# Outer products of a linear attention on half of the matmul array, and a new order of matmuls in a feed-forward block

## The chip, the cores and the metric

One NeuronCore of a Trainium2 chip runs the whole program. Its engines work through their own instruction queues side by side: PE (TensorE, the matmul array; PEld are its weight loads), ACT (ScalarE), DVE (VectorE), POOL (GpSimd) and SP, which here only issues DMAs. The metric is the time of one execution on the device in microseconds; before the change the median of three runs is 203.42 us (203.08 to 203.95).

## What is computed

A recurrent attention with decay feeds a two-layer network with a Mish activation.

```python
# q, k, v: (4, 8, 768, 64) fp32 (batch, heads, tokens, head size)
gamma = 1.0 - 2.0 ** (-5.0 - np.arange(H))
for t in range(S):
    state = gamma * state + outer(k[:, :, t], v[:, :, t])      # 64 x 64 per batch and head
    y[:, :, t] = scale * q[:, :, t] @ state
x = y.transpose(0, 2, 1, 3).reshape(3072, 512)
h = x @ w_in                                                    # (512, 2048)
out = (h * np.tanh(softplus(h))) @ w_out                        # (2048, 512), fp32 result
```

## The kernel before

The 3072 tokens are cut into 24 chunks of 128 (six to a batch). Two chunks make a block; the first block has four, so there are eleven blocks, 0 to 10. Of a chunk the attention is computed in a closed form, with the powers of the decay folded into q and v when they are cast to 16 bits:

- *scores* (`scores`, line 393): k times q within the chunk, per head, 16 matmuls for two chunks; `mask` (line 399) multiplies them by a triangle on DVE and gives `am`.
- *present* (line 443): v times `am`, the part of the output that comes from the chunk's own tokens. Each matmul has 64 weight columns, so that two heads lie in the two halves of the array.
- *outer* (line 407): k times v, summed over the chunk's tokens. Two heads lie side by side in one 128x128 product, of which only the two 64x64 squares on the diagonal are wanted; four matmuls a chunk.
- *state*: `state_sum` (line 419) adds the state of the chunk before on DVE, `state_decay` (line 424) multiplies by `gcm`, which holds the decay on the diagonal squares and zero elsewhere. The state is thus a 128x512 tile per chunk with zeros off the diagonal, and goes into
- *past* (line 433) as 128x128 weights: the part of the output that comes from earlier chunks, four matmuls a chunk.

`y_two` runs past and then present for the two chunks of a block into one PSUM tile `y_ps`, and ACT casts the result to `xt` (line 489), the input of the network.

Block 0 and the second product of block 1 are computed plainly, matmul by matmul, with the attention of the next block put between by a dictionary of steps (`plan` in `first_block`, `plan_of`). From there on both matrix products of a block go by a scheme of seven products in place of eight on quarters of the matrices: `g1_seven` (first product, with Mish; half of its units are seven-product quarters, line 639, half are `plain` units, line 663) and `seven` (second product, line 734). Both keep partial sums in three PSUM tiles `pb`, `px`, `pe`; `snap` copies one out on ACT (lines 646, 740), `plus` and `done` add on DVE (lines 656, 748). `x_sums`, `sums_a`, `sums_b` and `sums_c` form the sums of inputs on DVE that the scheme wants. A plain unit computes two columns of 128 and its Mish follows it at once.

The order of all instructions is the order in which the program is written; every engine takes its own in that order. The attention of the next block (nb) is put between by named steps: `steps_of(blk)` gives for each name the work that is issued there. In `g1_seven` the steps are p2, u2, p6, p7, p4, h2 and end, in `seven` m1, m2, m7 and m3. Before the change, p2 holds the next block's outer products (`outer_next`), the first sum and, on POOL, its decay; p7 the second sum; m2 the second decay; h2 the scores; m7 `y_two`. The casts of q and v on POOL, the loads of k by POOL's DMA queue (`bring_k`) and the transposing loads by SP (`turn_by_dma`) run two blocks ahead. `gate` is a small copy on POOL that makes the work behind it wait for sums on DVE.

PSUM is split into two pools: `mm` has four tiles for the network, `at` two for scores, outer products and `y_ps`.

Of the kernel before, what the change touches and what calls it, by code (L numbers as in the profile page):

```python
# [16 lines left out]
def kernel(  # L17
# [64 lines left out]
    tri = cpool.tile([P, C], FP32, name="tri")  # L82
    gcm = cpool.tile([P, HP, P], FP32, name="gcm")
    warm = cpool.tile([P, 1], FP32, name="warm")
    gate_t = cpool.tile([P, 1], FP16, name="gate")
# [19 lines left out]
    for h in range(H):  # L105
        o = 64 * (h % 2)
        nc.vector.memset(gcm[o:o + 64, h // 2, o:o + 64], float(gamma[h] ** C))

    win_ap = moe_w_in.rearrange("(bp p) f -> p bp f", p=P)
# [3 lines left out]
    raw, k16s, v16s, t16s, kts, amf = {}, {}, {}, {}, {}, {}  # L113
    loaded, cast, qkts, ats, ams, states, us, ys, sus = {}, {}, {}, {}, {}, {}, {}, {}, {}
    xts, gts, wins, wouts, wtmps = {}, {}, {}, {}, {}
# [10 lines left out]
    def room(g):  # L126
        loaded[g] = [
            lpool.tile([P, H, D], FP32, name=nm + "f", tag=nm + "f", bufs=4 if nm == "q" else 6)
            if g < BRING or nm != "k" else None for nm in "qkv"]
# [93 lines left out]
    def load_two(nm, s, half):  # L223
        t = lpool.tile([P, HP, R, D], FP32, name=nm + "f", tag=nm + "f", bufs=6)
# [179 lines left out]
    def outer(g, u_ps):  # L404
        _, k16, v16, _ = cast[g]
        for i in range(HP):
            nc.tensor.matmul(  # L407
                u_ps[:, i], k16[:, 2 * i:2 * i + 2], v16[:, 2 * i:2 * i + 2],
                start=True, stop=True)
        us[g] = u_ps  # L410

    def state_sum(g):
        u_ps = us.pop(g)
        if g % NCH == 0:
            states[g] = stp.tile([P, HP, P], FP16, name="st")
            nc.vector.tensor_tensor(states[g], u_ps, gcm, op=ALU.mult)
        else:
            sus[g] = stp.tile([P, HP, P], FP32, name="su")
            nc.vector.tensor_tensor(sus[g], u_ps, states[g - 1], op=ALU.add)  # L419

    def state_decay(g, by):
        if g in sus:
            states[g] = stp.tile([P, HP, P], FP16, name="st")
            by.tensor_tensor(states[g], sus.pop(g), gcm, op=ALU.mult)  # L424

    def state(g):
        state_sum(g)
        state_decay(g, nc.vector)

    def past(g, y, fresh, pairs=range(HP)):  # L430
        st, qt = states[g - 1], qkts[g][0]
        for i in pairs:
            nc.tensor.matmul(  # L433
                y(i), st[:, i], qt[:, i], start=fresh(i), stop=False,
                skip_group_check=True)

    def present(g, y, fresh, pairs=range(HP)):
        am = ams[g]
        v16 = cast[g][2]
        for i in pairs:  # L440
            for hh in range(2):
                o = 64 * hh
                nc.tensor.matmul(  # L443
                    y(i)[o:o + 64], v16[:, 2 * i + hh], am[:, hh, i],
                    start=fresh(i), stop=True, skip_group_check=True)

# [5 lines left out]
    def scores_one(g):  # L452
        scores(g)
        mask(g)

    def outer_state(g):
        outer(g, atps.tile([P, 2, HP, P], FP32, name="u_ps", tag="at")[:, 0])
        state(g)

# [9 lines left out]
    def outer_two(blk):  # L469
        a = first[blk]  # L470
        u_ps = atps.tile([P, 2, HP, P], FP32, name="u_ps", tag="at")
        for j in range(2):
            if not last_of_batch(a + j):
                outer(a + j, u_ps[:, j])
        for j in range(2):
            if not last_of_batch(a + j):
                state(a + j)

    def y_two(blk):
        a = first[blk]  # L480
        y_ps = atps.tile([P, HP, 2, C], FP32, name="y_ps", tag="at")
        inter = a % NCH > 0
        if inter:
            past(a, lambda i: y_ps[:, i, 0], lambda i: i % 2 == 0)
        past(a + 1, lambda i: y_ps[:, i, 1], lambda i: not inter and i % 2 == 0)
        for j in range(2):
            present(a + j, lambda i: y_ps[:, i, j], lambda i: False)
        xts[blk] = xtp.tile([P, HP, TB], FP16, name="xt")
        nc.scalar.copy(  # L489
            xts[blk][:, :, :2 * C], y_ps.rearrange("p i j c -> p i (j c)"))  # L490
# [125 lines left out]

    def g1_seven(blk, steps, sum_first=False):
        n = NBP // 2
# [40 lines left out]
        def plain(s, half):  # L659
            h_ps = mmps.tile([P, 2, 2 * P], FP32, name="h_ps", tag="mm")  # L660
            for j in range(2):
                for bp in range(NBP):
                    nc.tensor.matmul(  # L663
                        h_ps[:, j], win(s, 2 * half + j, bp), xt(blk, bp),
                        start=bp == 0, stop=bp == NBP - 1)
            fb = s * FPS + 2 * half
            nc.scalar.activation(gt[:, fb:fb + 2], h_ps, AF.Mish, scale=inv_boost3)  # L667
# [33 lines left out]
        plain(1, 1)  # L701
        step("h2")
        plain(3, 1)
        step("end")
# [9 lines left out]
    def seven(blk, steps, last):  # L714
# [51 lines left out]
        sums_c(blk)  # L766
        mm(pe, s(1), t(1), True)
        m5 = snap(pe)
        mm(px, s(3), t(3))
# [41 lines left out]
    def first_block():  # L811
# [72 lines left out]
        for s in range(1, NSL):  # L884
# [47 lines left out]

    def outer_next(blk):
        a = first[blk]
        u_ps = atps.tile([P, 2, HP, P], FP32, name="u_ps", tag="at")
        for j in range(2):
            if not last_of_batch(a + j):
                outer(a + j, u_ps[:, j])

    def sum_next(blk, j):  # L940
        if not last_of_batch(first[blk] + j):
            state_sum(first[blk] + j)

    def decay_next(blk, j):
        state_decay(first[blk] + j, nc.gpsimd)

# [49 lines left out]
    for blk in range(1, len(BLOCKS)):  # L996
        if blk >= SEVEN:
            steps = steps_of(blk)
            g1_seven(blk, steps, blk + 1 < len(BLOCKS) and not last_of_batch(first[blk + 1] + 1))
            seven(blk, steps, blk + 1 == len(BLOCKS))  # L1000
            continue
# [47 lines left out]
```

## Time and profile before

| what | us |
|---|---|
| median of three runs | 203.42 |
| the profiled execution's own time | 204.0 |
| its span, from the first to the last instruction | 202.2 |
| PE busy in it | 193.7 |
| DVE busy | 143.9 |
| ACT busy | 102.6 |
| POOL busy | 82.4 |
| outer products, line 407, 64 matmuls, busy | 5.2 |
| present, line 443, 160 matmuls, busy | 6.4 |
| sums of states on DVE, line 419, 13 | 8.9 |
| decays on POOL, line 424, 11 | 13.9 |

The profile is one execution. A busy time is the union of an engine's instructions; a matmul is shown with its full length, though the next one starts before it ends, so the spacing of starts says what a matmul costs. In the view of the chain, each piece is named by the engine and the line that the end of the program was waiting for at that time. In the timeline, a row gives the start of a merged piece, its length, the engine, the line and the operation, what is written and read, and how many instructions lie in it; square brackets name idle time ahead of it and what ended it.

### The profile page before, as it was taken

How to read it: one execution, taken by the hardware profiler on the slowest of the kernel's cores; microseconds unless marked ns; L12 is line 12 of the kernel's file. 1: busy time of each engine (PE TensorE's matmuls, PEld its weight loads, DVE VectorE, ACT ScalarE, POOL GpSimd, SP SyncE). 2: the span in 40 equal slices, each digit the busy share in tenths (PEclk: the TensorE clock that was granted, in tenths of full speed). 3: DMA queues.
4: the chain of work that ended last, by engine and by line, in shares of the span. 5: the costliest groups of instructions: out<-in, count | busy, mean ns of one | idle time of the engine just before them, and what ended most of it. 6: DMA issues, size and time to landing. Idle time of an engine off the chain costs nothing.

```text
span 202.2 us, 5401 instructions
## 1 busy us (share of the span) xinstructions
PE 193.7 (96%) x2239; PEld 153.0 (76%) x2239; DVE 143.9 (71%) x271; ACT 102.6 (51%) x183; POOL 82.4 (41%) x99
## 2 busy tenths in 40 slices
PE   6897999989999999999999999999999999999993
PEld 2455544445865888988988988988988988989982
DVE  2777693969848687588696696787696696596552
ACT  2363664151960572673573573563663753753840
POOL 4072000617645347646608629626609716200000
PEclk9999999999999999999999999999999999999999
DMA  5999999999899999999991998999992992200202
GB/s 163 303 312 357 386 386 305 270 255 194 150 116 273 253 201 202 144 176 211 188 183 49 151 165 174 167 172 156 209 200 62 186 136 56 105 3 28 80 26 78
DMA packets 95896, 36.55 MB, mean 181 GB/s; under 512 B 82304, under 2 KB 89984, under 8 KB 95872
## 3 DMA queue, kind: packets, MB, share of 16 engines
q1 hardware_dynamic: 75968, 33.30, 73.1%
q0 software_dynamic: 16640, 2.10, 16.4%
q10 hardware_dynamic: 3264, 0.82, 2.3%
q8 instruction: 17, 0.28, 0.6%
q14 instruction: 7, 0.06, 0.1%
HBM read 27.30 MB, written 6.29 MB: 166 GB/s over the span
## 4 chain that ended last, share of the span: by engine, by line
PE 80%; DMA 8%; DVE 6%; ACT 2%; issue 1%; SPq 0%; DVEq 0%
PE o_ps L734 28%; PE h_ps L663 18%; PE h_ps L639 16%; DMA wt<-in_moe_w_out_dram 6%; PE o_ps L526 6%; PE y_ps L443 3%; PE at L393 3%; DMA qfirst<-in_q_dram 2%; PE y_ps L433 2%; PE u_ps L407 2%; DVE tmat L558 1%; PE h_ps L807 1%; ACT xt L489 1%; DVE tmat L560 1%; DVE tmat L559 1%
## 5 line engine op out<-in xcount | busy, mean ns | idle before, releaser
L663 PE MATMUL h_ps<-xt,win 128*128 128x256 f16 x320 | 41.2, 273 | 0.0
L330 POOL TENSOR_TENSOR qk<-qf,qvs 128x512 f16<-128x512 f32 x20 | 24.0, 1199 | 25.5 <-DMA qf<-in_q_dram 25.3
L663 PEld LDWEIGHTS <-win 128*128 128x128 f16 x320 | 29.4, 98 | 3.6
L734 PEld LDWEIGHTS <-gsum 128*128 128x128 f16 x288 | 27.5, 98 | 3.8
L656 DVE TENSOR_TENSOR hsum<-h_ps,hsnap 128x512 f32<-128x512 f32 x30 | 19.8, 688 | 13.7 <-PE h_ps L639 11.4
L399 DVE TENSOR_TENSOR am<-at,tri 128x1024 f16<-128x1024 f32 x20 | 24.2, 1217 | 3.6 <-PE at L393 3.6
L667 ACT ACTIVATE g<-h_ps 128x512 f16<-128x512 f32 x40 | 23.8, 594 | 5.6 <-PE h_ps L663 5.5
L646 ACT COPY hsnap<-h_ps 128x512 f32<-128x512 f32 x30 | 16.6, 588 | 17.6 <-PE h_ps L639 17.6
L734 PE MATMUL o_ps<-tmat,gsum 128*128 128x256 f16 x216 | 25.1, 273 | 0.0
L345 POOL TENSOR_TENSOR v<-vf,qvs 128x512 f16<-128x512 f32 x20 | 21.3, 1063 | 5.2 <-DMA vf<-in_v_dram 5.2
L734 PEld LDWEIGHTS <-g 128*128 128x128 f16 x216 | 21.1, 98 | 2.4
L748 DVE TENSOR_TENSOR osb<-o_ps,snap 128x256 f32<-128x256 f32 x27 | 11.4, 424 | 16.0 <-PE o_ps L734 11.3
L526 PE MATMUL o_ps<-wout,g 128*128 128x512 f16 x96 | 22.7, 379 | 0.0
L489 ACT CAST xt<-y_ps 128x1024 f16<-128x1024 f32 x10 | 10.1, 1012 | 21.9 <-PE y_ps L443 21.9
L650 ACT ACTIVATE g<-hsum 128x512 f16<-128x512 f32 x30 | 18.7, 634 | 4.0 <-DVE hsum L656 4.0
L740 ACT COPY snap<-o_ps 128x256 f32<-128x256 f32 x27 | 10.1, 373 | 19.4 <-PE o_ps L734 19.4
L639 PEld LDWEIGHTS <-wsum 128*128 128x128 f16 x320 | 19.1, 98 | 0.5
L734 PE MATMUL o_ps<-wout,g 128*128 128x256 f16 x144 | 17.2, 273 | 0.0
L354 POOL COPY gate<-gsum 128x1 f16<-128x1 f16 x8 | 1.5, 183 | 37.9 <-DVE gsum L708 37.9
L639 PE MATMUL h_ps<-xsum,wsum 128*128 128x128 f16 x240 | 16.6, 219 | 0.0
L424 POOL TENSOR_TENSOR st<-su,gcm 128x512 f16<-128x512 f32 x11 | 13.9, 1267 | 6.1 <-DVE su L419 6.1
L639 PEld LDWEIGHTS <-win 128*128 128x128 f16 x240 | 15.1, 98 | 1.5 <-issue 0.8
(97 smaller groups left out, 294.0 us busy)
## 6 DMA issues: line engine op xcount, KB each, us to landing
vf<-in_v_dram SPq DMA_DIRECT2D x23, 256.0 KB, 5.7
out_dram<-osb SPq DMA_DIRECT2D x22, 256.0 KB, 4.9
qf<-in_q_dram SPq DMA_DIRECT2D x19, 256.0 KB, 5.5
wt<-in_moe_w_out_dram SPq DMA_DIRECT2D x3, 1024.0 KB, 9.2
wi<-in_moe_w_in_dram SPq DMA_DIRECT2D x4, 512.0 KB, 7.4
wi<-in_moe_w_in_dram SPq DMA_DIRECT2D x2, 1024.0 KB, 11.7
qk<-in_k_dram POOLq DMA_DIRECT2D x16, 128.0 KB, 5.4
kf<-in_k_dram SPq DMA_DIRECT2D x7, 256.0 KB, 6.0
```

What stands on the lines that cost most here:

```text
L330: nc.gpsimd.tensor_tensor(room16(g)[0], loaded[g][0], qs.unsqueeze(2).broadcast_to((P, H, D)), op=ALU.mult)
L345: nc.gpsimd.tensor_tensor(room16(g)[2], loaded[g][2], vs.unsqueeze(2).broadcast_to((P, H, D)), op=ALU.mult)
L399: nc.vector.tensor_tensor(am, ats.pop(g), tri.unsqueeze(1).unsqueeze(1).broadcast_to((P, 2, HP, C)), op=ALU.mult)
L424: by.tensor_tensor(states[g], sus.pop(g), gcm, op=ALU.mult)
L526: nc.tensor.matmul(o_ps, gts[blk, fb][:, t * P:(t + 1) * P], wouts[s][:, f, cols], start=(fb == 0), stop=(fb == NFB - 1))
L639: nc.tensor.matmul(h_ps[:, f], w(f, d), x(d), start=first and f == 0 and d == 0, stop=d == n - 1, skip_group_check=True)
L646: nc.scalar.copy(x, h_ps)
L650: nc.scalar.activation(gt[:, 2 * i * FPS:(2 * i + 1) * FPS, j * P:(j + 1) * P], h, AF.Mish, scale=inv_boost3)
L656: nc.vector.tensor_tensor(h, h_ps, x, op=ALU.add)
L663: nc.tensor.matmul(h_ps[:, j], win(s, 2 * half + j, bp), xt(blk, bp), start=bp == 0, stop=bp == NBP - 1)
L667: nc.scalar.activation(gt[:, fb:fb + 2], h_ps, AF.Mish, scale=inv_boost3)
L734: nc.tensor.matmul(o_ps, x(f), w(f), start=first and f == 0, stop=f == n - 1, skip_group_check=True)
```

## The change

Three things change together.

*Outer products and states.* `outer` computes each head alone: eight matmuls a chunk with 64 weight columns and 64 moving columns, the two heads of a pair in the two halves of the array. The result is compact, 128x256 with no zeros. `state_sum` and `state_decay` work on this compact form; `gcv` holds the decay as one column per pair of heads. `spread_state` then has ACT copy the two halves of partitions into a 128x512 tile (`stx`, three of them, whose zeros off the diagonal are set once at the start). One chunk, the fifth, keeps the wide form (`outer_wide`).

*Where they stand.* `y_two` now runs present first, then the outer products of the block's second chunk and of the next block's first (`outer_two`, `handed_on`; the last chunk of a batch has none), then past. The sums and decays follow in the steps of the next block's `g1_seven` and `seven`: sum and decay of one chunk at p2 with its spread at p7, sum of the other at p7, decay at m2 and spread at a new step m5. In block 0's plan `y_two` and in block 1's plan `outer_state` both compute the outer product of the seventh chunk.

*The first product.* `g1_seven` now issues a plain unit behind each pair of seven-product quarters; the Mish of a plain unit is issued later than its matmuls. The load buffers of k go from six to four.

```diff
     def outer(g, u_ps):
         _, k16, v16, _ = cast[g]
         for i in range(HP):
+            for hh in range(2):
+                nc.tensor.matmul(
+                    u_ps[64 * hh:64 * hh + 64, i], k16[:, 2 * i + hh], v16[:, 2 * i + hh],
+                    start=i == 0, stop=True, skip_group_check=True)
+        us[g] = u_ps
+
+    def state_sum(g):
+        u_ps = us.pop(g)
+        if g % NCH == 0:
+            stcs[g] = stp.tile([P, HP, D], FP16, name="stc", tag="stc")
+            nc.vector.tensor_tensor(stcs[g], u_ps, decay, op=ALU.mult)
+        else:
+            sus[g] = stp.tile([P, HP, D], FP32, name="suc", tag="suc")
+            nc.vector.tensor_tensor(sus[g], u_ps, stcs[g - 1], op=ALU.add)
+
+    def state_decay(g, by):
+        if g in sus:
+            stcs[g] = stp.tile([P, HP, D], FP16, name="stc", tag="stc")
+            by.tensor_tensor(stcs[g], sus.pop(g), decay, op=ALU.mult)
+
+    def spread_state(g):
+        states[g] = stx[g % 3]
+        for hh in range(2):
+            o = slice(64 * hh, 64 * hh + 64)
+            nc.scalar.copy(states[g][o, :, o], stcs[g][o])
...
     def y_two(blk):
         a = first[blk]
         y_ps = atps.tile([P, HP, 2, C], FP32, name="y_ps", tag="at")
-        inter = a % NCH > 0
-        if inter:
-            past(a, lambda i: y_ps[:, i, 0], lambda i: i % 2 == 0)
-        past(a + 1, lambda i: y_ps[:, i, 1], lambda i: not inter and i % 2 == 0)
         for j in range(2):
-            present(a + j, lambda i: y_ps[:, i, j], lambda i: False)
+            present(a + j, lambda i: y_ps[:, i, j], j == 0)
+        outer_two(blk)
+        for j in range(2):
+            if (a + j) % NCH > 0:
+                past(a + j, lambda i: y_ps[:, i, j])
...
         step("p2")
-        if sum_first:
-            mm(px, s(2), t(2))
-            u2 = snap(px)
+        h0 = plain(1, 0)
+        mm(px, s(2), t(2))
+        mish_of(0, 0, c11)
+        u2 = snap(px)
         mm(pe, s(1), t(1), True)
         m5 = snap(pe)
-        if not sum_first:
-            mm(px, s(2), t(2))
-            u2 = snap(px)
+        mish_plain(1, 0, h0)
         step("u2")
-        mish_of(0, 0, c11)
         step("p6")
-        plain(1, 0)
+        h1 = plain(3, 0)
         mm(px, s(3), t(3))
         c22 = plus(px, m5)
         mm(pe, s(4), b(1, 1))
         c12 = plus(pe, u2)
+        mish_plain(3, 0, h1)
         mish_of(1, 1, c22)
         mish_of(0, 1, c12)
         step("p7")
-        plain(3, 0)
+        h2 = plain(1, 1)
+        mish_plain(1, 1, h2)
         mm(px, a(1, 1), t(4))
         mish_of(1, 0, px)
         step("p4")
-        plain(1, 1)
         step("h2")
-        plain(3, 1)
+        h3 = plain(3, 1)
+        mish_plain(3, 1, h3)
         step("end")
...
-            28: [(outer_state, CPB), (casts, CPB + 2), (turn_and_load, CPB + 2), (cast_q, CPB + 3)],
+            28: [(outer_wide, CPB), (casts, CPB + 2), (turn_and_load, CPB + 2), (cast_q, CPB + 3)],
...
-            "p2": [*then((gate_x, blk), (cast_q, a)), *only((outer_next, nb), (sum_next, nb, 0),
-                   (decay_next, nb, 0)), (cast_v, a), (bring_k, a + 1)],
+            "p2": [*then((gate_x, blk), (cast_q, a)), (sum_next, a - 3), (decay_next, a - 3),
+                   (cast_v, a), (bring_k, a + 1)],
...
-            "p7": [(store_due, 2), *only((sum_next, nb, 1)), (sums_a, blk, slice(0, FPS))],
+            "p7": [(store_due, 2), (sum_next, a - 2), (spread_next, a - 3), (sums_a, blk, slice(0, FPS))],
...
-            "m2": [*only((gate_g, blk), (decay_next, nb, 1)), (cast_q, a + 1), (cast_v, a + 1),
+            "m2": [*only((gate_g, blk), (decay_next, a - 2)), (cast_q, a + 1), (cast_v, a + 1),
                    (bring_k, a + 2), *only((mask, a - 1)), (turn_and_load, a + 1)],
+            "m5": only((spread_next, a - 2)),
             "m7": only((y_two, nb)),
...
-                12: [(outer_two, blk + 1), (cast_v, a + 1), (bring_k, a + 2),
+                12: [(outer_state, first[blk] + 2), (cast_v, a + 1), (bring_k, a + 2),
                      (turn_and_load, a + 1)],
```

More of the change, by code (lines that the diff above doesn't have):

```diff
@@ L83 @@
     gcm = cpool.tile([P, HP, P], FP32, name="gcm")
+    gcv = cpool.tile([P, HP], FP32, name="gcv")
+    stx = [cpool.tile([P, HP, P], FP16, name=f"stx{i}") for i in range(3)]
     warm = cpool.tile([P, 1], FP32, name="warm")
@@ L107 @@
         nc.vector.memset(gcm[o:o + 64, h // 2, o:o + 64], float(gamma[h] ** C))
+        nc.vector.memset(gcv[o:o + 64, h // 2:h // 2 + 1], float(gamma[h] ** C))
+    decay = gcv.unsqueeze(2).broadcast_to((P, HP, D))
+    for t in stx:
+        nc.gpsimd.memset(t, 0.0)
     win_ap = moe_w_in.rearrange("(bp p) f -> p bp f", p=P)
@@ L223, in load_two @@
     def load_two(nm, s, half):
[L224 removed]
+        t = lpool.tile([P, HP, R, D], FP32, name=nm + "f", tag=nm + "f", bufs=6 if nm == "v" else 4)
         nc.sync.dma_start(
@@ L428, in state, with outer_wide, past, present @@
         state_decay(g, nc.vector)
-    def past(g, y, fresh, pairs=range(HP)):
+        spread_state(g)
+    def outer_wide(g):
+        _, k16, v16, _ = cast[g]
+        u_ps = u_tile()[:, 0]
+        for i in range(HP):
+            nc.tensor.matmul(
+                u_ps[:, i], k16[:, 2 * i:2 * i + 2], v16[:, 2 * i:2 * i + 2],
+                start=True, stop=True)
+        su = stp.tile([P, HP, P], FP32, name="su", bufs=1)
+        nc.vector.tensor_tensor(su, u_ps, states[g - 1], op=ALU.add)
+        states[g] = stp.tile([P, HP, P], FP16, name="st")
+        nc.vector.tensor_tensor(states[g], su, gcm, op=ALU.mult)
+    def past(g, y):
         st, qt = states[g - 1], qkts[g][0]
-        for i in pairs:
+        for i in range(HP):
             nc.tensor.matmul(
-                y(i), st[:, i], qt[:, i], start=fresh(i), stop=False,
-                skip_group_check=True)
-    def present(g, y, fresh, pairs=range(HP)):
+                y(i), st[:, i], qt[:, i], start=False, stop=True, skip_group_check=True)
+    def present(g, y, fresh):
         am = ams[g]
         v16 = cast[g][2]
-        for i in pairs:
+        for i in range(HP):
             for hh in range(2):
@@ L444, in present @@
                     y(i)[o:o + 64], v16[:, 2 * i + hh], am[:, hh, i],
-                    start=fresh(i), stop=True, skip_group_check=True)
+                    start=fresh and i % 2 == 0, stop=g % NCH == 0, skip_group_check=True)
     def last_of_batch(g):
@@ L454, in scores_one, with u_tile, handed_on @@
         mask(g)
+    def u_tile():
+        return atps.tile([P, 2, HP, P], FP32, name="u_ps", tag="at")
     def outer_state(g):
-        outer(g, atps.tile([P, 2, HP, P], FP32, name="u_ps", tag="at")[:, 0])
+        outer(g, u_tile()[:, 0, :, :D])
         state(g)
+    def handed_on(blk):
+        return [g for g in (first[blk] + 1, first[blk] + 2) if g < NCK and not last_of_batch(g)]
     def scores_two(blk):
@@ L469, in outer_two @@
     def outer_two(blk):
[L470 to L477, printed above, removed]
+        gs = handed_on(blk)
+        if gs:
+            u_ps = u_tile()
+        for j, g in enumerate(gs):
+            outer(g, u_ps[:, j, :, :D])
     def y_two(blk):
@@ L615, in x_sums, with g1_seven @@
         nc.vector.tensor_tensor(t[:, 3], b[1][0], t[:, 1], op=sub)
-    def g1_seven(blk, steps, sum_first=False):
+    def g1_seven(blk, steps):
         n = NBP // 2
@@ L665, in plain, with mish_plain @@
                         start=bp == 0, stop=bp == NBP - 1)
+            return h_ps
+        def mish_plain(s, half, h_ps):
             fb = s * FPS + 2 * half
@@ L767, in seven @@
         mm(pe, s(1), t(1), True)
+        step("m5")
         m5 = snap(pe)
@@ L931, in turn_and_load, with sum_next, decay_next, spread_next @@
             load_to(g + 3)
[L933 to L945, printed above, removed]
+    def sum_next(g):
+        if g in us:
+            state_sum(g)
+    def decay_next(g):
+        state_decay(g, nc.gpsimd)
+    def spread_next(g):
+        if g in stcs:
+            spread_state(g)
     def gate_x(blk):
@@ L998 @@
             steps = steps_of(blk)
-            g1_seven(blk, steps, blk + 1 < len(BLOCKS) and not last_of_batch(first[blk + 1] + 1))
+            g1_seven(blk, steps)
             seven(blk, steps, blk + 1 == len(BLOCKS))
```

12 lines of the change are left out of this document (2 added, 10 removed).

## The prediction

> **What bounds the kernel now.** I read the page first: engine totals, the clock row, the chain that ended last.
>
> ```profile
> span 202.2 us, 5401 instructions
> PE 193.7 (96%) x2239; PEld 153.0 (76%) x2239; DVE 143.9 (71%) x271; ACT 102.6 (51%) x183; POOL 82.4 (41%) x99
> PEclk9999999999999999999999999999999999999999
> PE 80%; DMA 8%; DVE 6%; ACT 2%; issue 1%; SPq 0%; DVEq 0%
> ```
>
> PE is busy 96% at an undisturbed clock and holds 80% of the chain. A busy PE may still wait inside its pieces, so the second view is the chain in order of time over one block of the steady part (start, length, what).
>
> ```profile
> 142.64 0.45 PE u_ps L407 x8
> 143.09 0.89 PE h_ps L639 x16
> 143.98 0.87 PE h_ps L663 x8
> 144.85 0.89 PE h_ps L639 x16
> ...
> 153.84 0.22 PE y_ps L433 x4
> 154.06 0.57 PE y_ps L443 x16
> 154.63 1.85 PE o_ps L734 x16
> ```
>
> Every piece is PE, and every piece is its count times one step: 0.89/16 = 0.056 us for a full-array matmul of 128 columns, 0.87/8 = 0.109 us for 256. From block 2 on there is no waiting to remove; only PE steps count. The outer products (L407) cost 0.45/8 = 0.056 us each, 0.223 us a chunk. The half-array products (L443) step differently: 16 in 0.57 us. The timeline, cut after 153.99 us at ever later ends, shows why.
>
> ```profile
> 153.99 0.11 PEld L443 LDWEIGHTS <-v 128*64 128x64 f16 x2
> 153.99 0.14 PEld L443 LDWEIGHTS <-v 128*64 128x64 f16 x4
> 153.99 0.25 PE L443 MATMUL y_ps<-am,v 128*64 128x128 f16 x2
> 153.99 0.30 PE L443 MATMUL y_ps<-am,v 128*64 128x128 f16 x4
> 153.99 0.64 PE L443 MATMUL y_ps<-am,v 128*64 128x128 f16 x16
> ```
>
> Two start together (x2: both halves of the array), and the rest of each row's length is the next pair: 0.25 to 0.30 us for the second pair, which follows with one lag of a first load, and (0.64 - 0.30)/6 = 0.056 us a pair after that. The second pair of weight loads starts 0.14 - 0.11 = about 0.03 us after the first: a 64-column load takes 0.03 us, both halves at once. A pair of 128 columns thus costs as much as one full-array matmul, for the same product. Going into this mode and out costs about 0.1 us each: past starts at 153.68 on PE, and its four take 0.22, so 0.09 us pass before 153.99; the 16 of 1.85 us should be 16 x 0.109 = 1.75.
>
> ```profile
> 153.68 0.39 PE L433 MATMUL y_ps<-qkt,st 128*128 128x128 f16 x4
> ```
>
> **The change, part by part.** (a) *Outer products.* Four full matmuls of 128 columns become eight of 64 columns on 64-column weights, in four pairs. A pair streams half of the 128 columns, 0.056/2 = 0.028 us, and its load (0.03) runs beside the pair before: 4 x 0.029 = 0.116 us a chunk in place of 0.223, so -0.107. Ends: 0.116 if streaming and loading keep overlapping, and 0.223 (4 x 0.056, the pair's price at twice the columns) if nothing is gained. I take 0.116, since both the stream and the load row are near 0.03. The Trainium skill (TensorE: Matmul & The Clock Gate, LDWEIGHTS) gives columns over 1.2 GHz for a load, an estimate of 0.053 us for 64 columns; by that, a pair stays at 0.053 and the sum below ends near +0.3 us; the rows, with loads 0.03 apart, differ, and they decide. In the steady blocks, the products leave the first product (2 x 0.223) and come back behind present, already in half-array mode: the mode switch that stood between past and present now stands ahead of present, the one behind present stands ahead of past. Count unchanged, nothing added. Twelve chunks (9 to 22 without the last of a batch) move so: 12 x -0.107 = -1.28 us.
>
> (b) *First product's order.* In blocks with one outer product, a piece of 16 matmuls takes 0.95 us, not 0.89: PE waits for the snapshot of u2, which is copied just ahead.
>
> ```profile
> 85.35 0.95 PE h_ps L639 x16
> ...
> 188.90 0.95 PE h_ps L639 x16
> ```
>
> There are four (85, 131, 175, 189 us). With plain units between the pairs, the snapshot has 0.87 us more: 4 x -0.06 = -0.24. What is late next is in (d).
>
> (c) *Blocks 0 to 2, where PE waits for xt.*
>
> ```profile
> 48.57 1.21 DVE L399 TENSOR_TENSOR am<-at,tri 128x1024 f16<-128x1024 f32 x1
> 48.66 1.05 POOL L345 TENSOR_TENSOR v<-vf,qvs 128x512 f16<-128x512 f32 x1 [0.56 <-DMA vf<-in_v_dram]
> ...
> 49.40 0.45 PE y_ps L433 x8
> 49.84 0.59 PE y_ps L443 x16
> ...
> 50.45 1.02 ACT xt L489
> ...
> 51.52 1.50 PE h_ps L639 x24
> ...
> 66.28 1.02 ACT xt L489
> ...
> 67.34 1.05 PE h_ps L639 x16
> ```
>
> Here the cast of xt is in the chain: whatever lengthens y_two is paid in full. Block 1's y_two begins at 49.23 on PE (0.17 before its piece of the chain, as 153.68 stands to 153.84), and past (0.45) covered the wait for the mask that ends at 48.57 + 1.21 = 49.78. With present first, chunk 4's four pairs end near 49.6; chunk 5 waits to 49.83 and ends at 50.05; then comes an outer product of chunk 6, which block 1's plan computes once more (0.12; its v ends at 49.71, cover 0.3 us), the switch (0.12), and past (0.45) to 50.72. Its last matmul starts near 50.67; a matmul's 0.22 us (0.39 - 3 x 0.056) and 0.04 on, at 50.93, xt can start, in place of 50.45: +0.48. In block 1 the plan's two outer products (0.45) become one, with two switches of 0.1 and a first load of 0.05: 0.38, -0.06. Its y_two holds two outer products more and ends with past: present 0.09 + 0.47, outer 0.23, switch 0.12, past 0.17 to its last start, 0.26 to the cast: xt starts 1.34 after y_two's begin and not 1.00 (past 0.22, switch 0.09, present 0.43, 0.26): +0.34. Block 2's first product then lacks those two (-0.45). Together +0.48 - 0.06 + 0.34 - 0.45 = +0.31.
>
> (d) *States and spreading.* DVE's sum halves (681 to about 420 ns), POOL's decay too (1267 to about 650): both off the chain. ScalarE gets two SBUF copies of 64x256 a chunk. A 512-wide SBUF cast takes 622 ns, and 588 and 373 ns at 512 and 256 columns from PSUM make 215 ns for 256 columns: 0.41 us each, some 0.37 from start to start.
>
> ```profile
> L341 ACT CAST qk<-kf 128x512 f16<-128x512 f32 x4 | 2.5, 622 | 8.4 <-DMA qf<-in_q_dram 4.8 <-DMA kf<-in_k_dram 3.6
> L646 ACT COPY hsnap<-h_ps 128x512 f32<-128x512 f32 x30 | 16.6, 588 | 17.6 <-PE h_ps L639 17.6
> L740 ACT COPY snap<-o_ps 128x256 f32<-128x256 f32 x27 | 10.1, 373 | 19.4 <-PE o_ps L734 19.4
> L419 DVE TENSOR_TENSOR su<-u_ps,st 128x512 f32<-128x512 f32 x13 | 8.9, 683 | 0.4 <-PE u_ps L407 0.4
> L424 POOL TENSOR_TENSOR st<-su,gcm 128x512 f16<-128x512 f32 x11 | 13.9, 1267 | 6.1 <-DVE su L419 6.1
> ```
>
> One pair stands at p7 ahead of three Mish calls, which the second product waits for. Before, in the same block:
>
> ```profile
> 146.13 1.23 ACT L650 ACTIVATE g<-hsum 128x512 f16<-128x512 f32 x2 [0.42 <-DVE hsum L656]
> 147.27 0.58 ACT L667 ACTIVATE g<-h_ps 128x512 f16<-128x512 f32 x1
> 147.74 0.59 ACT L650 ACTIVATE g<-h_ps 128x512 f16<-128x512 f32 x1
> 149.51 0.60 ACT L667 ACTIVATE g<-h_ps 128x512 f16<-128x512 f32 x1 [0.69 <-PE h_ps L663]
> 149.31 1.91 PE L734 MATMUL o_ps<-wout,g 128*128 128x256 f16 x16
> 144.69 0.61 PE L639 MATMUL h_ps<-xsum,wsum 128*128 128x128 f16 x8
> 145.41 1.29 DVE L656 TENSOR_TENSOR hsum<-h_ps,hsnap 128x512 f32<-128x512 f32 x2 [1.27 <-PE h_ps L639]
> 151.66 1.22 DVE L399 TENSOR_TENSOR am<-at,tri 128x1024 f16<-128x1024 f32 x1
> ```
>
> The two Mish calls on sums step 0.57, the others 0.47. Let S be the second product's start (149.31 before). The sums' last matmul moves 0.87 us nearer to S, so these calls start at 146.13 - 149.31 + 0.87 = S - 2.31 and end their steps at S - 1.17; the spread pair reaches S - 0.43, the plain unit's Mish S + 0.05, and the one of quadrant (1,0) is done at S + 0.69. The second group of matmuls reads it at S + 8 x 0.109 = S + 0.87: cover 0.18 us. The last Mish is done at S + 1.2, read at S + 1.53. Nothing is paid, but this is the thinnest cover: without it, each 0.1 us costs 0.1 in each of six blocks. The sum at p7 must free the u tile for the second scores: DVE's c22 starts 0.72 us after its first matmul (as 145.41 after 144.69 before), c12 and the sum 0.6 later each (1.29 for two, less one's 0.69), so the sum of 0.42 is done at 2.39 with its signal; PE wants it after two products (0.89), a plain unit (0.87), one product (0.45), the switch and the first scores (0.33): 2.54, cover 0.15. DVE's sums of g and the masks behind them run some 0.6 later against S, because the last Mish is 0.4 later and the first mask now stands ahead of the last sums; the second mask, done at 151.66 + 1.22 = S + 3.57, comes to S + 4.15, and present reads it at S + 4.37 + 0.29: cover 0.5. POOL's gate opens those 0.6 later, its decay takes 0.6 less, so the q cast behind it, and SP's transposing load that waits for the cast, stay where they were. The pair at m5 delays m5's snapshot by 0.8; a product, present, outer and past stand ahead of its next use (over 2 us).
>
> (e) *The rest at nothing*: constants set while POOL and DVE wait for the first loads; two kf buffers less, whose earlier tiles are cast long before.
>
> **Sum:** -1.28 - 0.24 + 0.31 = -1.2 us against the profiled execution, 204.0 us (span 202.2): 202.8. That execution lies 0.6 above the median of the runs shown, 203.42; from the median, 202.2 us, -0.6%.
>
> **Rivals.** *No gain from halves* (the columns' two halves take turns, 0.223 a chunk, for 16 narrow chunks: 12 steady, 2 in block 1's y_two, chunk 6 twice): -1.2 + 16 x 0.107 = +0.5, 203.9. For it: no row has 64 moving columns. Against it: pairs start together. The Trainium skill (TensorEngine Tiling (Array Packing), Instruction Overhead) speaks against this change: it states some 60 cycles for each matmul and advises against tiling a dimension that is small already. By 25 ns for each of eight, an estimate from that page, a chunk would be 0.2 us and the kernel at 203.6; starts of a pair together in the rows speak against it.
>
> *Small waits* (the u tile or the Mish of (1,0) 0.1 us late in six to eight blocks): +0.6 to +0.8, so 202.8 to 203.0. Against it stand covers of 0.15 and 0.18, which are thin.
>
> *Slower: ScalarE late at p7.* If a spread copy steps at 0.7 and not 0.37 (strided 16-bit rows, no row shows one), the pair takes 1.4; minus cover 0.18, (1,0) is 0.48 late in six blocks: -1.2 + 2.9 = +1.7, 205.1. It decides from 0.56 a copy. Against: the 512-wide cast, double in size, takes 0.62 in whole.
>
> **How the numbers follow.** Chances: forecast 0.5; no gain 0.17; small waits 0.17; late ScalarE or a wait like it 0.16. Predicted 202.2. Low: -0.6 for block 0's waits if they are hidden, 201.6; high: between no gain (203.9) and 205.1, 204.4. The change that a measurement can tell from none is about 0.5%, 1.0 us: the forecast lies only 0.2 beyond, so a tenth of it counts as the same. Faster 0.46, same 0.35, slower 0.19.
>
> **What would show it.** Narrow outer rows with eight starts in 0.12 us a chunk (0.22: no gain); a first product of 0.45 us less in two-chunk blocks, y_two 0.23 more; all 16-matmul pieces at 0.89; L489 in block 0 near 50.9 us. Wrong if PE shows waits at the second product's ninth matmul, at the second scores, or at past (POOL's decay late), or if the spread copies take over 0.5 us.

## The result and the profile after

The changed kernel takes 202.73 us (median of 20 runs, 202.4 to 203.69), the kernel before beside it 203.5 us (20 runs): a ratio of 0.9966, 95% interval 0.9954 to 0.9978, which is 0.7 us less (0.45 to 0.94). The forecast was 1.2 us less. The profiled execution took 203.19 us. From the page of the changed kernel, the engine totals and the chain's shares:

```profile
PE 192.6 (96%) x2307; PEld 151.6 (75%) x2307; DVE 138.7 (69%) x278; ACT 112.9 (56%) x213; POOL 76.9 (38%) x103
PE 78%; DMA 8%; DVE 8%; ACT 2%; issue 1%; SPq 0%; DVEq 0%
```

PE still sets the end. ACT has 10 us more to do and DVE and POOL 5 us less each; neither the spread copies nor the compact sums and decays stand on the chain. The chain of the changed kernel in order of time (start, length, what), one block of the steady part:

```profile
141.51 0.89 PE h_ps L666 x16
142.40 0.87 PE h_ps L690 x8
...
153.15 0.57 PE y_ps L469 x16
153.72 0.25 PE u_ps L415 x16
153.97 0.33 PE y_ps L460 x4
154.30 1.80 PE o_ps L764 x16
156.10 0.89 PE h_ps L666 x16
...
198.15 0.42 DVE osb L776
```

The outer products have left the first product (no u_ps among the h_ps pieces) and stand between present (L469) and past (L460): 16 matmuls, two chunks, in 0.25 us. The block takes 156.10 - 141.51 = 14.59 us; before it was 14.73 (141.75 to 156.48). All four pieces of 0.95 us are 0.89 now. The timeline of the changed kernel, cut after 153.55 us at two ends, shows the steps of the narrow matmuls (start, length, engine, operation, count):

```profile
153.55 0.39 PE L415 MATMUL u_ps<-v,qk 128*64 128x64 f16 x14
153.55 0.42 PE L415 MATMUL u_ps<-v,qk 128*64 128x64 f16 x16
```

Two matmuls more add 0.03 us (0.42 - 0.39): they start together, and the pairs step at 0.25/8 = 0.031 us. The Trainium skill (TensorE: Matmul & The Clock Gate, Measured speedup vs the span model) gives about 4 ns for each further tile of the array that works beside the first; the trace agrees, with 3 or 4 ns between the single starts of a pair.

The chain of the changed kernel in blocks 0 and 1, where the cast of xt lies on it:

```profile
42.42 0.40 PE at L400 x8
...
48.49 1.15 DVE am L406
49.68 0.41 PE y_ps L469 x8
50.09 0.13 PE u_ps L415 x6
50.22 0.57 PE y_ps L460 x8
50.81 1.02 ACT xt L516
51.87 1.05 PE h_ps L666 x16
...
66.89 1.02 ACT xt L516
67.95 1.05 PE h_ps L666 x16
```

The mask (DVE, L406) is on the chain now, with present behind it. In block 0 the cast starts 50.81 - 42.42 = 8.39 us after the scores of the fifth chunk (chunk 4 where they are counted from 0); before it was 7.85. The scores' own start depends on early loads and moves by up to a microsecond from run to run (41.7 to 42.7 in the chains of this study), so the stretches below are counted from landmarks in each kernel's own chain, and not from zero.

| from the chain, us | scores of the fifth chunk to block 1's first product | to block 2's first product | to the end of the last output copy | sum |
|---|---|---|---|---|
| before | 8.92 | 15.82 | 132.15 | 156.89 |
| changed | 9.45 | 16.08 | 130.62 | 156.15 |
| difference | +0.53 | +0.26 | -1.53 | -0.74 |

Two of the first row's landmarks, 51.52 and 67.34, stand in the prediction; the other two, from the chain of the kernel before:

```profile
42.60 0.40 PE at L393 x8
...
199.06 0.43 DVE osb L746
```

-0.74 agrees with the measured 0.7. The forecast, cut in the same way, was +0.48, +0.28 and -1.97. Blocks 0 and 1 came out as worked; 0.44 us of the gain from block 2 on is missing.

### The profile page after: what moved, and what is told of

Same layout as the page of the kernel before. It is cut to its first block, busy times and chain, and to the rows that moved or that the text cites. A ratio compares the mean times of both kernels' runs of the same rounds, so it can differ in the third digit from the quotient of the medians.

```text
span 201.3 us, 5579 instructions
## 1 busy us (share of the span) xinstructions
PE 192.6 (96%) x2307; PEld 151.6 (75%) x2307; DVE 138.7 (69%) x278; ACT 112.9 (56%) x213; POOL 76.9 (38%) x103
## 4 chain that ended last, share of the span: by engine, by line
PE 78%; DMA 8%; DVE 8%; ACT 2%; issue 1%; SPq 0%; DVEq 0%
PE o_ps L764 27%; PE h_ps L690 18%; PE h_ps L666 16%; DMA wt<-in_moe_w_out_dram 6%; PE o_ps L553 4%; PE y_ps L469 3%; PE at L400 3%; PE y_ps L460 2%; DMA qfirst<-in_q_dram 2%; PE u_ps L415 1%; DVE tmat L585 1%; ACT xt L516 1%; PE h_ps L838 1%; DVE st L455 1%; DVE tmat L587 1%
## 5 line engine op out<-in xcount | busy, mean ns | idle before, releaser
L337 POOL TENSOR_TENSOR qk<-qf,qvs 128x512 f16<-128x512 f32 x20 | 21.5, 1077 | 25.8 <-DMA qf<-in_q_dram 25.7
L406 DVE TENSOR_TENSOR am<-at,tri 128x1024 f16<-128x1024 f32 x20 | 24.3, 1217 | 3.5 <-PE at L400 3.5
L352 POOL TENSOR_TENSOR v<-vf,qvs 128x512 f16<-128x512 f32 x20 | 23.5, 1173 | 5.1 <-DMA vf<-in_v_dram 5.1
L697 ACT ACTIVATE g<-h_ps 128x512 f16<-128x512 f32 x40 | 23.0, 603 | 0.7 <-PE h_ps L690 0.6
L438 ACT COPY stx<-stc 64x256 f16<-64x256 f16 x30 | 12.0, 400 | 7.5 <-DVE stc L424 5.5
```

Of the source, the lines that this page charges most:

```text
L337: nc.gpsimd.tensor_tensor(room16(g)[0], loaded[g][0], qs.unsqueeze(2).broadcast_to((P, H, D)), op=ALU.mult)
L352: nc.gpsimd.tensor_tensor(room16(g)[2], loaded[g][2], vs.unsqueeze(2).broadcast_to((P, H, D)), op=ALU.mult)
L406: nc.vector.tensor_tensor(am, ats.pop(g), tri.unsqueeze(1).unsqueeze(1).broadcast_to((P, 2, HP, C)), op=ALU.mult)
```

## The experiments

The theory: PE's steps set the time, the gain is the narrow outer product times the number of chunks, and the small waits removed and added explain the rest. Rivals: the half-size sums matter and not the matmuls; the order of the first product alone brings the gain; a late ScalarE at p7 has eaten the rest; or block 0 has.

### Outer products on the whole array again, in the new places

```diff
         for i in range(HP):
-            for hh in range(2):
-                nc.tensor.matmul(
-                    u_ps[64 * hh:64 * hh + 64, i], k16[:, 2 * i + hh], v16[:, 2 * i + hh],
-                    start=i == 0, stop=True, skip_group_check=True)
+            nc.tensor.matmul(
+                u_ps[:, i], k16[:, 2 * i:2 * i + 2], v16[:, 2 * i:2 * i + 2],
+                start=True, stop=True)
...
-            stcs[g] = stp.tile([P, HP, D], FP16, name="stc", tag="stc")
-            by.tensor_tensor(stcs[g], sus.pop(g), decay, op=ALU.mult)
+            states[g] = stp.tile([P, HP, P], FP16, name="st")
+            by.tensor_tensor(states[g], sus.pop(g), gcm, op=ALU.mult)
...
-        spread_state(g)
```

> The changed kernel with the outer products on the full array again (four matmuls of 128 columns, state 128x512, no spread copies, sums and decays on the wide tile), in their new places behind present. Theory (the time is the sum of PE's steps): 14 chunks cost 0.223 and not 0.125 us, +1.37; chunk 6 once more in block 0 +0.1; in block 1's plan two mode switches fewer, -0.13: +1.3 us against the changed kernel, +0.6 against the kernel before. Rival (the gain comes from smaller sums on DVE and POOL, or the spread copies on ScalarE hold it back): within 0.3 us of the changed kernel, or faster.

Measured: 204.99 us, ratio 1.0075 (1.0048 to 1.0102). From block 2 on it takes 132.72 us, 2.10 more than the changed kernel, and not 1.3. Its chain at the scores of a block, and DVE's timeline there:

```profile
148.51 0.68 PE at L397 x16
...
155.11 0.55 PE u_ps L411 x8
```

```profile
148.06 0.68 DVE L420 TENSOR_TENSOR st<-u_ps,gcm 128x512 f16<-128x512 f32 x1
```

The scores take 0.68 us where they take 0.55 in the changed kernel: the wide sum holds the PSUM tile until 148.06 + 0.68 = 148.74, and the second scores want that tile. This happens in eight blocks, 0.13 us each, 1.0 us. Twelve wide chunks at 0.223 in place of 0.125 add 1.2, and 0.09 us that the changed kernel waits for another DVE sum (s4, the last sum of g, of which more below) fall away: 2.1 in all. So against the changed kernel the rival that names the sums has half the difference. Against the kernel before it has none of the gain: there the sums were as wide, and the scores took 0.55 too. From the chain before:

```profile
147.94 0.55 PE at L393 x16
```

There a plain unit of 0.87 us more stood between the sum at p7 and the scores, and the new order has moved it ahead of that sum. The short sum is thus what the new order needs to stay free of a wait, and not a gain of its own. The sum is 0.27 us longer here (0.68 against the 0.41 of the changed kernel) and PE waits 0.13, so the cover in the changed kernel is 0.14; the prediction had 0.15.

### The outer products at p2, on half arrays

```diff
-        outer_two(blk)
+        if blk == 1:
+            outer_two(blk)
...
-            "p2": [*then((gate_x, blk), (cast_q, a)), (sum_next, a - 3), (decay_next, a - 3),
+            "p2": [(outer_two, blk), *then((gate_x, blk), (cast_q, a)), (sum_next, a - 3), (decay_next, a - 3),
```

> The changed kernel with the half-array outer products of blocks 2 to 9 taken out of y_two and issued at p2 of the first product, among full-array matmuls. Theory: eight blocks pay two mode switches more, 0.13 in and 0.10 out: +1.85 us against the changed kernel, +1.15 against before, so that half arrays lose at that place. Rival (a mode switch overlaps other work): +0.0 to +0.3.

Measured: 204.76 us, ratio 1.0071 (1.0044 to 1.0098); from block 1's first product to the end 149.03 us, 2.33 more than the changed kernel. Its chain:

```profile
142.97 0.24 PE u_ps L415 x8
143.22 0.98 PE h_ps L691 x8
...
153.64 1.41 DVE gsum L743
...
155.10 1.92 PE o_ps L765 x16
```

One narrow chunk now takes 0.24 us and the piece behind it 0.98 in place of 0.87. In the single starts of the trace, 0.093 us pass on the way into the half-array mode, the second pair comes 0.05 us behind the first where a step is 0.031, 0.10 pass on the way out, and the first plain matmul behind takes 0.01 more: 0.23 in each of eight blocks, 1.8 us. The rest, 0.5 us, is the wait for s4 (`gsum`, L743) in the last rows: in the two blocks whose past has four matmuls only, PE reaches the product that reads s4 0.25 us earlier than in the changed kernel, and waits 0.29 us in place of 0.045. In this kernel the halves gain only beside other half-array work.

### The first product in the old order

```diff
         step("p2")
-        h0 = plain(1, 0)
-        mm(px, s(2), t(2))
-        mish_of(0, 0, c11)
-        u2 = snap(px)
+        if sum_first:
+            mm(px, s(2), t(2))
+            u2 = snap(px)
         mm(pe, s(1), t(1), True)
         m5 = snap(pe)
-        mish_plain(1, 0, h0)
+        if not sum_first:
+            mm(px, s(2), t(2))
+            u2 = snap(px)
...
-            g1_seven(blk, steps)
+            g1_seven(blk, steps, blk + 1 < len(BLOCKS) and not last_of_batch(first[blk + 1] + 1))
```

> The changed kernel with the first product in the order of before, including its rule that u2's product comes first where the next block has two outer products. Theory: with the outer products gone from that place, in five blocks u2's matmuls come 0.89 us after the block's start, while the snapshot of px that they overwrite is done at 1.28: +0.39 each; in four blocks the wait of 0.06 comes back: +2.2 us against the changed kernel, +1.5 against before. Rival (the order is worth its four waits alone): +0.24 against the changed kernel.

Measured: 204.48 us, ratio 1.0064 (1.0039 to 1.0089); from block 2 on 2.05 us more than the changed kernel. Its chain in a block with the product of u2 first:

```profile
142.03 0.46 PE h_ps L666 x8
142.52 0.59 ACT hsnap L673
...
143.15 1.05 PE h_ps L666 x16
```

PE waits for ACT's copy of m1, since u2's product goes into the same PSUM tile: 0.39 us in five blocks. With four waits of 0.058 for u2's copy, and without the two for s4, that is 2.1. Before the change two wide outer products (0.45 us) stood at this place and covered the copy, which the prediction had not seen: it took them away and priced only their absence. The new order hides the copy behind a plain unit, so the two parts of the change need each other.

### The old order with m5's product always first

```diff
-            g1_seven(blk, steps, blk + 1 < len(BLOCKS) and not last_of_batch(first[blk + 1] + 1))
+            g1_seven(blk, steps)
```

> The changed kernel with the first product in the order of before, m5's product always first, so that px has one product more time. Theory: the wait of 0.39 us of the other rule is gone, the wait of 0.06 for u2's snapshot stands in all nine blocks from 2 on: +0.5 us against the changed kernel, -0.2 against before. Rival (order is worth nothing): +0.0.

Measured: 203.22 us, ratio 0.9988 (0.9975 to 1.0002); from block 2 on 0.39 us more than the changed kernel. The diff is against the run above. Its chain has the longer piece, as the kernel before had in four blocks:

```profile
144.32 0.95 PE h_ps L666 x16
```

Nine blocks at 0.058, less the 0.09 at s4 that this order hides, make 0.43. This is what the new order is worth against the best of the old ones: some 0.4 of the 1.5 us, the rest is the outer products.

### The spread copies twice at p7

This run does the two ScalarE copies of step p7 twice over and computes nothing else in another way.

```diff
-            "p7": [(store_due, 2), (sum_next, a - 2), (spread_next, a - 3), (sums_a, blk, slice(0, FPS))],
+            "p7": [(store_due, 2), (sum_next, a - 2), (spread_next, a - 3), (spread_next, a - 3), (sums_a, blk, slice(0, FPS))],
```

> The changed kernel with the spread copies at p7 done twice (0.83 us more on ScalarE in six blocks). Theory (the cover there is 0.1 to 0.15 us): the second product stops for about 0.7 us in each of six blocks, +4.2 us against the changed kernel. Rival (ScalarE is idle 44% of the time and takes it in): +0.0 to +0.3.

Measured: 207.84 us, ratio 1.021 (1.0179 to 1.0241); from block 2 on 4.81 us more. ScalarE's timeline of this run, and then of the changed kernel:

```profile
74.02 1.67 ACT L438 COPY stx<-stc 64x256 f16<-64x256 f16 x4
75.71 0.60 ACT L697 ACTIVATE g<-h_ps 128x512 f16<-128x512 f32 x1
```

```profile
162.05 0.80 ACT L438 COPY stx<-stc 64x256 f16<-64x256 f16 x2
162.88 0.60 ACT L697 ACTIVATE g<-h_ps 128x512 f16<-128x512 f32 x1
163.37 0.59 ACT L677 ACTIVATE g<-h_ps 128x512 f16<-128x512 f32 x1
```

The pair takes 0.80 us, 0.40 a copy (the prediction took 0.41 for one, 0.37 from start to start). The Trainium skill (ScalarE: Activation LUTs, What ACT_TABLE_LOAD costs) states 186 ns and 0.833 ns for each column for an ACTIVATE with immediate scale and bias; by that, an estimate for 256 columns is 0.40 us, and the trace agrees, though it calls these copies COPY. The Mish behind the copies starts 1.69 us after the first of them (75.71 - 74.02) in place of 0.83 (162.88 - 162.05), 0.86 later, and PE then stops twice in the second product, 0.52 us at its seventh matmul and 0.26 at its ninth, in six blocks: 6 x 0.78 = 4.7. The chain of this run goes over ScalarE up to that ninth matmul (32 of 40 are left):

```profile
76.85 3.67 PE o_ps L764 x32
```

All but 0.08 us of each extra pair is paid. The cover that (d) put at 0.18 is thus about 0.08, and the changed kernel lies just on the good side of it: it has no stop at these matmuls.

### Block 0: no outer product twice, and past first

```diff
-        outer_two(blk)
+        if blk > 1:
+            outer_two(blk)
```

> The changed kernel without the outer product of chunk 6 in block 1's y_two, which block 1's plan computes again. Theory: it lies in the path to xt, 4 pairs of 0.031: -0.13 us, so the cast of xt starts 0.13 earlier against the end of the masks; in the time it can't be told from the changed kernel.

Measured: 202.73 us, ratio 0.9974 (0.9959 to 0.9989), where the changed kernel has 0.9966; the medians can't tell this step. Its chain:

```profile
42.05 0.40 PE at L400 x8
...
50.34 1.02 ACT xt L517
```

The cast starts 8.29 us behind the scores in place of 8.39: 0.10 of the 0.54 lost in block 0 belong to the chunk that is computed twice. The second run adds to this the old order of past and present in this one place:

```diff
+        if blk == 1:
+            for j in range(2):
+                past(a + j, lambda i: y_ps[:, i, j], j == 0)
+            for j in range(2):
+                present(a + j, lambda i: y_ps[:, i, j], False)
+        else:
...
```

> As that, and block 1's y_two runs past first again, so that past covers the wait for the second mask. Theory: the 0.53 us that block 0 lost come back: -0.5 us against the changed kernel, -1.2 against before (ratio 0.994). Rival (that loss was an earlier or later DMA in the profiled run and not the order): no difference to the changed kernel, ratio 0.9966.

Measured: 202.30 us, ratio 0.9948 (0.9931 to 0.9966). Its chain:

```profile
42.31 0.40 PE at L400 x8
...
50.15 1.02 ACT xt L522
51.21 1.05 PE h_ps L672 x16
```

The cast is at 7.84 again, and from the scores to block 1's first product it takes 8.90 us (before 8.92, changed 9.45). Everything behind is as in the changed kernel (146.71 us to the end, against 146.70). So past, in the place where the mask is waited for, is worth 0.45, as (c) says. The same kernel, run once more beside the last experiment:

> The kernel with past first in block 1's attention and no outer product twice, run once more on the same chip as the last one. Both theories: ratio to before 0.995 as in its first run, stretch from block 1's first product to block 10's last 131.15 us; block 0 takes about 0.55 us less than in the changed kernel, counted from the start of the scores of chunk 4.

Measured: 202.42 us, ratio 0.9946 (0.9926 to 0.9966), stretches of 8.91 and 146.71 us. This version is faster than the kernel before, and by its landmarks 0.53 us shorter than the changed kernel; the intervals of the two ratios still overlap.

### Block 1: the cast of xt ahead of the outer products

In block 1 PE also waits for the cast of xt (66.89 in the chain after). This run takes the version with past first and moves the outer products of that one y_two behind the cast.

```diff
-            outer_two(blk)
+            if blk > 2:
+                outer_two(blk)
...
             xts[blk][:, :, :2 * C], y_ps.rearrange("p i j c -> p i (j c)"))
+        if blk == 2:
+            outer_two(blk)
```

> As that, and block 2's y_two runs present, past, the cast of xt, and only then the two outer products, in the time in which PE waits for xt. Theory: the path to xt loses 0.25 us of outer products, PE's idle 0.4 us takes them and 0.24 us of mode switches in: -0.2 us more, -0.7 against the changed kernel, -1.4 against before (ratio 0.993).

Measured: 202.62 us, ratio 0.9964 (0.9945 to 0.9984): no gain. From block 1's first product to the end it takes 146.71 us, the same to 0.01. PE's stop of 0.40 us ahead of block 2 is gone. Its chain and DVE's timeline show what took its place:

```profile
66.38 0.37 PE u_ps L415 x16
66.76 0.97 PE o_ps L562 x4
...
71.26 1.01 PE h_ps L675 x16
72.27 0.93 PE h_ps L699 x8
```

```profile
67.76 0.69 DVE L571 COPY osb<-o_ps 128x512 f32<-128x512 f32 x1 [3.08 <-PE o_ps L562]
68.37 0.28 DVE L648 TENSOR_TENSOR xsum<-xt 128x256 f16<-128x256 f16 x1
```

Behind past, the outer products need a switch of their own: 0.37 us for the two chunks in place of 0.25, and 0.97 in place of 0.86 behind them. And they push block 1's last four matmuls, and so DVE's copy of their result, behind which the sums of xt stand in DVE's queue; block 2's first product then waits 0.17 us (1.01 and 0.93 for 0.89 and 0.87). Is the second half of that reading right? The last run issues the sums of xt ahead of the copy:

```diff
-                14: [(y_two, blk + 1)]}
+                14: [(y_two, blk + 1), (x_sums, blk + 1)]}
...
-        x_sums(blk + 1)
```

> As in the run that casts xt of block 2 ahead of the outer products, and the four sums of xt are issued on DVE right behind that cast, ahead of the copy of block 1's last output tile. Theory (that copy, pushed behind the outer products, had held up the sums of xt by 0.67 us and cost 0.17 in block 2's first product): the sums start with the cast's end, near 24.95 us after the scores of chunk 4 have started, PE stops nowhere in block 2's first product, and the stretch from block 1's first product to block 10's last is about 0.2 us shorter than in the run with past first alone (131.15 to about 130.95); ratio to before about 0.994. Rival (what the cast gains is lost at another place, whatever DVE does first): the stretch stays at 131.15 and the ratio at 0.995.

Measured: 202.29 us, ratio 0.9941 (0.9922 to 0.9961). DVE's timeline:

```profile
67.37 0.29 DVE L648 TENSOR_TENSOR xsum<-xt 128x256 f16<-128x256 f16 x1 [2.96 <-ACT xt L523]
...
68.31 0.68 DVE L571 COPY osb<-o_ps 128x512 f32<-128x512 f32 x1
```

The sums start with the end of the cast, 24.90 us after the scores of the fifth chunk (which start at 42.47 in this run; 25.63 in the run above, from 42.74), PE stops nowhere in block 2's first product, and from block 2's y_two to the end it takes 132.71 us in place of 132.87: 0.16 of the 0.2 expected. The whole stretch from block 1's first product is shorter by only 0.06, since in this run PE stops for 0.11 us between the two scores of block 1, ahead of the edit; why, no run here shows. Its median can't be told from that of the version with past first.

The stretches of all kernels, from their chains (as in the table above):

| us | to block 1 | to block 2 | to the end | median | ratio |
|---|---|---|---|---|---|
| changed | 9.45 | 16.08 | 130.62 | 202.73 | 0.9966 |
| wide outer products | 9.56 | 16.15 | 132.72 | 204.99 | 1.0075 |
| outer products at p2 | 9.46 | 15.83 | 133.20 | 204.76 | 1.0071 |
| old order | 9.50 | 16.09 | 132.67 | 204.48 | 1.0064 |
| old order, m5 first | 9.46 | 16.08 | 131.01 | 203.22 | 0.9988 |
| spread twice | 9.47 | 16.08 | 135.43 | 207.84 | 1.0210 |
| nothing twice | 9.36 | 16.08 | 130.62 | 202.73 | 0.9974 |
| past first | 8.90 | 16.08 | 130.63 | 202.30 | 0.9948 |
| past first, again | 8.91 | 16.08 | 130.63 | 202.42 | 0.9946 |
| cast ahead | 8.91 | 16.07 | 130.64 | 202.62 | 0.9964 |
| sums ahead | 8.91 | 16.18 | 130.47 | 202.29 | 0.9941 |

## Why the prediction was right, and where it was not

The direction and its mechanisms were right; the size was 1.2 where 0.7 was measured. The prediction held that a change under 1.0 us could not be told from none; with 20 runs of each kernel, 0.7 could. By its own steps:

**(a), the price of a narrow chunk.** Right in kind: the halves stream side by side. The term was 0.116 us and measured 0.125 (0.25 for two chunks): the pairs step at 0.031 and not at 0.029. Over the 12 chunks from block 2 on that is +0.11.

**(a) and (c), the count.** This is the step that failed most. "Twelve chunks move so" counted the products that come into y_two from block 2 on, and took as many out of p2 of those blocks, beside the two of block 2 that (c) takes out. Chunks 8 and 9 stood in p2 of block 2, and 9 is among the twelve already. Before, p2 of blocks 2 to 9 held 13 chunks in all, and after, the y_twos in the same blocks hold 12: so 13 x -0.223 + 12 x 0.125 = -1.40 and not -0.45 - 12 x 0.107 = -1.73. One wide chunk too many was taken off, 0.22 us. (The two that block 1's `y_two` takes over are 7 and 8; 7 had stood in block 1's plan, where (c) counts its leaving.)

**A wait not named.** (d) followed the masks to present and the sums to POOL's gate, but not s4, the subtraction `gsum<-g,gsum` that DVE computes behind the second mask. DVE's, POOL's and PE's timelines of the changed kernel:

```profile
152.64 1.49 DVE L742 TENSOR_TENSOR gsum<-g,gsum 128x1024 f16<-128x1024 f16 x1
```

```profile
152.54 1.03 POOL L352 TENSOR_TENSOR v<-vf,qvs 128x512 f16<-128x512 f32 x1
```

```profile
153.90 0.40 PE L460 MATMUL y_ps<-qkt,stx 128*128 128x128 f16 x4
154.19 0.61 PE L764 MATMUL o_ps<-wout,gsum 128*128 128x256 f16 x4
```

s4 is done at 154.13. In the single starts, past's last matmul starts 0.103 us ahead of the next product, where a step is 0.056. That is a wait of some 0.045 in two blocks, +0.09. The run with the outer products at p2 takes 0.25 us of cover away at this place and the wait grows by just that. In these two blocks past has four matmuls and s4 takes 1.49 us; in the others s4 takes 1.06 or 0.68, past has eight (0.22 us more), and PE finds s4 ready. The prediction also held that the q cast behind POOL's decay would stay where it was. But in these two blocks the chunk whose decay would stand at m2 is the first of a batch, which has none on POOL; the casts come earlier, and the cast of v now starts just ahead of s4. In the same block before the change POOL ran a decay there, and s4 took 0.68 us (from 152.79).

With (b)'s -0.24, the three terms give -1.40 + 0.09 - 0.24 = -1.55 from block 2 on, where -1.53 was measured.

**(b)** was right: all four waits for u2's copy are gone. What it left out is what the old outer products had covered at p2, 0.39 us in five blocks in the run with the old order; the new order covers it too, so nothing was paid.

**(c)** was right to 0.05 us: +0.53 for block 0 (+0.48) and +0.26 for block 1 (+0.28). The runs of block 0 part it: 0.10 for the chunk computed twice and 0.45 for present ahead of past.

**(d)** held, and one cover was thinner than worked. The Mish of (1,0) is done at S + 0.74 (163.37 + 0.59 with S = 163.22; forecast S + 0.69), and the run with the copies twice leaves a cover of 0.08 where 0.18 was taken; half of the difference is this later Mish. The u tile's cover came out at 0.14 (forecast 0.15).

**The rivals.** No gain from halves is refuted by the rows of L415. The Trainium skill's rule of some 60 cycles for each matmul (TensorEngine Tiling (Array Packing), Instruction Overhead) would give 0.2 us a chunk, an estimate with 25 ns for each of eight; 0.125 was measured, so two matmuls of a pair do not each pay it. The Trainium skill's price for a load (TensorE: Matmul & The Clock Gate, LDWEIGHTS), an estimate of 0.053 us for 64 columns, is not seen either: pairs step at 0.031 with a load for each matmul. Small waits came true in kind, at s4 and not where it was looked for, and with 0.09 us. ScalarE late at p7 was 0.08 us away, as the doubled copies show.

## What to carry to other kernels

When work moves from one place to another, count what leaves and what enters each block by name, chunk by chunk; the price of a step was good to 8 per cent here, and the count was off by one chunk. Half-array matmuls paid here where they stood beside others of the same mode; the same work alone in a stream of full-array matmuls lost 0.23 us to switches for a gain of 0.10 a chunk. And before work is taken out of a stream, ask what wait it has been covering: here the copy ahead of u2's product, and in block 0 the mask behind past. The same holds for an engine off the chain: with POOL's decay gone, a cast slid beside a sum that PE needs.

## What was not expected of the hardware

Four pairs of 64x64 outer products ran in 0.125 us, though each of the eight matmuls has its own weight load. A lone group of them inside full-array matmuls paid 0.09 us on the way in, 0.05 up to the second pair (a step is 0.03) and 0.10 on the way out. And the same subtraction on DVE, s4, differs within one run; its group in the changed kernel (ns, least, median and most):

```profile
L742 DVE TENSOR_TENSOR gsum<-g,gsum x9: 681/1060/1491, 79.2 to 194.4; 128x1024 f16<-128x1024 f16 x9
```

The two of 1.49 us are those that PE waited for. In all twelve traces of this study s4 takes 0.68 us where no cast or decay runs on GpSimd as it begins, and where one runs, s4 ends 0.55 to 0.57 us behind the end of that instruction, whenever that is: the cast of v above ends at 152.54 + 1.03 = 153.57, s4 at 154.13. So s4 seems to stand still until GpSimd is done. No run here moves the cast alone, so this cause is read from the rows and not tested.
